# A first strip by plain products, W_out half converted in SBUF, and pieces converted in pairs

## The chip, the cores and the metric

The kernel runs on one core of one Trainium2 chip. The metric is the device time of one execution in microseconds (us); the time of a kernel is the median over several runs. A core has five instruction streams that run beside each other: TensorE (PE; its weight loads are shown as PEld), VectorE (DVE), ScalarE (ACT), GpSimd (POOL) and SyncE (SP), and 16 DMA engines that move data between HBM and the on-chip memory SBUF. Matrix products land in PSUM.

## The reference

Attention without softmax, then a two-layer network whose hidden layer is squared after a ReLU:

```python
batch, n_heads, seq, head_dim = (8, 8, 576, 64)
kv = np.einsum('bhsd,bhse->bhde', k, v)
out = np.einsum('bhsd,bhde->bhse', q, kv)
rms = np.sqrt(np.mean(out * out, axis=-1, keepdims=True) + 1e-06)
attn = out / rms * g_norm
x = attn.transpose(0, 2, 1, 3).reshape(4608, 512)     # n_tokens, d_model
h = x @ w_in                                          # d_ff = 2048
r = np.maximum(h, 0.0)
return ((r * r) @ w_out).astype(np.float32)
```

q, k, v and g_norm are float32. `w_in` (512 x 2048) and `w_out` (2048 x 512) come as float64, 8.4 MB each, so the kernel converts them to float32 by integer operations on their words before it can use them.

## The kernel before, in words

**Tokens.** The 4608 tokens are 36 tiles of 128, worked on in 9 strips of 4 tiles (512 tokens). Attention for a pair of heads of one batch is a unit (b, p), 32 in all: `transposed_query` transposes q on PE (`t_ps`, and `tr_ps` for the 64 rows of two batches that are left over), `key_value` makes k^T v (`kv_ps`) and copies it to `kvd`. Per tile, `query` multiplies (`x_ps`), squares (`sq`), takes the root mean square on ACT and DVE and writes `x_n`; `features` transposes `x_n` (`xt_ps`) into `xT`.

**Products.** Both layers are done per strip by a scheme of 7 products of half-size blocks in place of 8 (Strassen-Winograd). `up(s, g, p)` is product p (order 1, 2, 6, 5, 7, 3, 4) of group g of four; it needs sums of blocks of W_in (slots of the SBUF tile `w_in`: 11, 21, 12, 22 and the sums S1, S2, S4) and of xT (`x_t`, made by `sums_x`). `combine` copies a PSUM bank to `snap` on ACT or adds it up on DVE; the hidden blocks are `gt`. `down(s, p, i)` is half i of product p of the second layer; its operand `w_blk` is streamed in blocks of 1 MB from `w_out`, a scratch tensor in HBM that holds the 7 block sums of the converted W_out. Banks: A (two buffers), B and C.

**Weights.** They arrive in 32 pieces of 512 KB (`raw`, three buffers), 16 of W_in and 16 of W_out. `convert_piece` makes two words per piece on ACT (L154, L169) and joins them in four DVE instructions (L155, L158, L164, L170), then asks for the next piece. The sums of W_in's blocks and of W_out's blocks are made on POOL (`sums_in` L183 and L174, `sums_out` L174); `sums_out` stores one row block of all 7 sums to `w_out` (L200).

**Order.** Each engine runs its instructions in the order in which the program writes them. The loop at the end writes strip 0's attention, then 28 `up` steps of strip 0 with the conversions spread between them by `convert(n)`; all conversions are written ahead of the first `down` of strip 0, and after that three `w_blk` loads. `attend(n)` spreads the next strip's attention over a strip's steps. All loads and stores but two tiny ones are issued from SP, in order; an issue whose buffer is not free holds up what stands behind it. All of that happens once; strips 1 to 8 only repeat `up`, `down` and attention.

Of the kernel before, what the change touches and what calls it, by code (L numbers as in the profile page):

```python
# [19 lines left out]
def kernel(  # L20
# [49 lines left out]
    qkv_pool = ctx.enter_context(tc.tile_pool(name="qkv", bufs=2))  # L70
    rest_pool = ctx.enter_context(tc.tile_pool(name="rest", bufs=NP))
# [6 lines left out]
    xc_pool = ctx.enter_context(tc.tile_pool(name="xc", bufs=1))  # L78
    snap_pool = ctx.enter_context(tc.tile_pool(name="snap", bufs=1))
    dram = ctx.enter_context(tc.tile_pool(name="dram", bufs=1, space=bass.MemoryType.DRAM))  # L80
    conv = ExitStack()
    raw_pool = conv.enter_context(tc.tile_pool(name="raw", bufs=3))
    wtmp = conv.enter_context(tc.tile_pool(name="wtmp", bufs=2))
    wt_pool = conv.enter_context(tc.tile_pool(name="wt", bufs=2))
# [7 lines left out]
    def load(b, p):  # L92
        hs = slice(2 * p, 2 * p + 2)
        half = slice(REST * (b % 2), REST * (b % 2 + 1))
        for n, src in (("k", k), ("v", v), ("q", q)):
            whole = src[b, hs, 0 : C * P].rearrange("h (sp c) d -> sp h c d", c=C)
            if n == "v":
                t = qkv_pool.tile([P, 2, C, D], FP32, name=n, tag=n)
                nc.sync.dma_start(out=t, in_=whole)
            else:  # L100

                t = qkv_pool.tile([P, C, 2, D], FP32, name=n, tag=n)
                for h in range(2):
                    nc.sync.dma_start(out=t[:, :, h, :], in_=whole[:, h])
# [10 lines left out]
    def load_next():  # L115
        u = next(to_load, None)
        if u is not None:
            load(*u)

    for _ in range(2):  # L120
        load_next()
# [26 lines left out]
    def convert_piece(i, dest):  # L148
# [27 lines left out]
    def piece_in(i):  # L176
        g, kc = divmod(i, NP)
        b = kc // KH * 2
        convert_piece(i, w_in[:, b : b + 2, kc % KH, ts(g, WN // 2)])

    def sums_in(g):
        a11, a21, a12, a22, s1, s2, s4 = (w_in[:, b, :, ts(g, WN // 2)] for b in range(7))
        nc.gpsimd.tensor_tensor(out=s1, in0=a21, in1=a22, op=ALU.add)  # L183
        minus(nc.gpsimd, s2, s1, a11)
        minus(nc.gpsimd, s4, a12, s2)
        minus(nc.gpsimd, a21, a11, a21)

    def piece_out(i):
        j, b = divmod(i, 2)
        if b == 0:  # L190
            wt[j] = wt_pool.tile([P, 7, DH], FP32, name="wt", tag="wt")
        convert_piece(NG * NP + i, wt[j][:, 2 * b : 2 * b + 2, :])

    def sums_out(j):
        b11, b12, b21, b22, t1, t2, t4 = (wt[j][:, b, :] for b in range(7))
        minus(nc.gpsimd, t1, b12, b11)
        minus(nc.gpsimd, t2, b22, t1)
        minus(nc.gpsimd, b12, b22, b12)
        minus(nc.gpsimd, t4, b21, t2)
        nc.sync.dma_start(out=w_out[:, :, j, :].rearrange("b p e -> p b e"), in_=wt.pop(j))  # L200

    conversions = []
    for g in range(NG):
        conversions += [(piece_in, NP * g + kc) for kc in range(NP)] + [(sums_in, g)]
    for j in range(FQ):
        conversions += [(piece_out, 2 * j), (piece_out, 2 * j + 1), (sums_out, j)]
# [8 lines left out]
    for _ in range(3):  # L215
        load_piece()

# [12 lines left out]
    def transposed_query(b, p):  # L230
# [6 lines left out]
        if b % 2:  # L237
            t = rest.pop(("q", b // 2, p))
# [3 lines left out]
            nc.vector.tensor_copy(qT["rest", b // 2, p], ps)  # L242

    def key_value(b, p):
# [3 lines left out]
        for c in range(C):  # L248
            nc.tensor.matmul(ps, lhsT=flat(tk[:, c]), rhs=tv[:, :, c, :], start=(c == 0), stop=False)  # L249
        nc.tensor.matmul(  # L250
            ps, lhsT=flat(rest["k", b // 2, p][half]), rhs=rest["v", b // 2, p][half], start=False, stop=True
# [6 lines left out]
        nc.vector.tensor_copy(d[D:P, D:P], ps[D:P, D:P])  # L258
        kvd[b, p] = d
        load_next()  # L260

    def query(n):
# [14 lines left out]
        sq = xn_pool.tile([P, d_model], FP32, name="sq", tag="sq")  # L277
# [40 lines left out]
    for b in range(B):  # L318
# [33 lines left out]
    B_OUT = {1: 0, 2: 2, 3: 3, 4: 6, 5: 4, 6: 5, 7: 1}  # L352
# [27 lines left out]

    def up(s, g, p):
# [6 lines left out]
        for i in range(2):  # L388
            product(p, i, lambda kc: w_in[:, A_IN[p], kc, ts(2 * g + i, P)], lambda kc: rhs[:, kc, :], KH)

        if (s, 1) not in gq:
            for q in (11, 12, 21, 22, 1):
                gq[s, q] = g_pool.tile([P, FQ, TH], FP32, name="gt", tag="gt")
        dest = {q: gq[s, q][:, 2 * g : 2 * g + 2, :] for q in (11, 12, 21, 22, 1)}

        def relu_squared(q):
            def f(b, a):
# [3 lines left out]
                if q == 12:  # L401
                    nc.vector.tensor_tensor(out=dest[1], in0=dest[12], in1=dest[22], op=ALU.add)
                    minus(nc.vector, dest[12], dest[11], dest[12])
# [8 lines left out]
    to_stream = iter([(s, p) for s in range(N_STRIP) for p in ORDER])  # L412
# [7 lines left out]
    def down(s, p, i):  # L420
# [8 lines left out]
        stream()  # L429
# [19 lines left out]
    for i in range(ready[0]):  # L449
        attend(i + 1)  # L450
        convert(i // 2 - 5)
    for s in range(N_STRIP):
        attend(ready[s])
        steps = [(1, up, (s, g, p)) for g in range(NG) for p in ORDER]
# [48 lines left out]
```

## Time and profile before

| what | value |
|---|---|
| time, median of 3 runs | 1126.4 us (1126.19 to 1126.85) |
| the profiled execution | 1126.69 us |
| its span, first to last instruction | 1124.9 us |
| PE busy | 1003.8 us (89%) |
| DVE, ACT, POOL busy | 461.5, 243.9, 61.2 us |
| moved by DMA | 128.75 MB |

The span leaves 1.8 us of the profiled execution outside. Busy shares are means over a start with conversions and a long stretch of strips, which have different limits, so the rows below are taken stretch by stretch. Windows and timelines count us from the start of the span.

### The profile page before, as it was taken

The page shows a single profiled execution, that of the slowest core. Times are in us where ns is not written, and L with a number is a line of the kernel's source. Part 1 is how long each engine was busy: PE and PEld are TensorE (multiplying, and loading weights), DVE is VectorE, ACT ScalarE, POOL GpSimd, SP SyncE. Part 2 cuts the span into 40 slices and gives each one's busy share as a digit, 9 for nine tenths or more (in the row PEclk, how much of TensorE's full clock was granted, in tenths as well). Part 3 has the DMA queues.
Part 4 walks back from the last instruction along what each step waited for, and adds up shares of the span by engine and source line. Part 5 has one row for each costly group of instructions (what it writes and reads, how often), then busy time and mean ns, then how long its engine had stood idle before and what let it go on. Part 6 is the DMA issues. An engine that isn't in the chain of part 4 may idle for free.

```text
span 1124.9 us, 12527 instructions
## 1 busy us (share of the span) xinstructions
PE 1003.8 (89%) x4960; PEld 878.9 (78%) x4960; DVE 461.5 (41%) x797; ACT 243.9 (22%) x454; POOL 61.2 (5%) x118
## 2 busy tenths in 40 slices
PE   3456920699999999999999999999999999999998
PEld 3345710588888888888888888888888888888887
DVE  0677788232442245234424342542253324512430
ACT  1423433012211221122103210321132112201200
POOL 0042235000000000000000000000000000000000
PEclk9888965799999999999999999999999999999999
DMA  7443468543334323422541354126402350044032
GB/s 187 108 130 109 132 206 270 187 164 102 87 104 137 116 71 116 145 71 64 148 169 47 74 151 156 45 63 186 161 18 64 122 178 1 11 154 135 1 112 75
DMA packets 123850, 128.75 MB, mean 114 GB/s; under 512 B 85008, under 2 KB 109584, under 8 KB 115728
## 3 DMA queue, kind: packets, MB, share of 16 engines
q1 hardware_dynamic: 123632, 127.95, 36.5%
q8 instruction: 39, 0.64, 0.2%
q14 instruction: 19, 0.16, 0.0%
q10 hardware_dynamic: 160, 0.00, 0.0%
HBM read 111.15 MB, written 16.78 MB: 114 GB/s over the span
## 4 chain that ended last, share of the span: by engine, by line
PE 84%; DVE 9%; DMA 3%; SPq 1%; POOL 1%; issue 1%; ACT 1%; DVEq 0%; POOLq 0%; ACTq 0%
PE ps_A L364 43%; PE ps_B L364 21%; PE ps_C L364 11%; PE x_ps L275 2%; PE kv_ps L249 2%; PE xt_ps L302 1%; PE t_ps L234 1%; PE kv_ps L250 1%; DMA raw<-in_moe_w_out_dram 1%; DVE w_c L155 1%; DVE w_c L158 1%; DVE w_in L170 1%; DVE gt L400 1%; DVE w_in L164 1%; DVE wt L164 1%
## 5 line engine op out<-in xcount | busy, mean ns | idle before, releaser
L364 PE MATMUL ps_A<-w_blk,gt 128*128 128x256 f32 x1152 | 259.1, 381 | 58.4 <-DMA w_blk<-w_out 58.4
L364 PEld LDWEIGHTS ps_A<-w_blk,gt 128*128 128x128 f32 x1152 | 218.0, 191 | 88.1 <-issue 58.8
L364 PE MATMUL ps_A<-x_t,w_in 128*128 128x256 f32 x864 | 206.6, 382 | 6.0 <-DVE w_in L170 5.3
L364 PEld LDWEIGHTS ps_A<-x_t,w_in 128*128 128x128 f32 x864 | 161.8, 190 | 29.7 <-DVE w_in L170 6.3
L364 PE MATMUL ps_B<-w_blk,gt 128*128 128x256 f32 x576 | 128.5, 379 | 0.0
L364 PEld LDWEIGHTS ps_B<-w_blk,gt 128*128 128x128 f32 x576 | 108.4, 190 | 14.3 <-issue 0.2
L174 DVE TENSOR_TENSOR gt<-gt 128x512 f32<-128x512 f32 (+1 forms) x54 | 69.0, 1279 | 87.4 <-PE ps_A L364 57.7
L374 ACT COPY snap<-ps_A 128x512 f32<-128x512 f32 x90 | 52.7, 585 | 203.0 <-PE ps_A L364 203.0
L364 PE MATMUL ps_A<-xT,w_in 128*128 128x256 f32 x288 | 74.1, 401 | 24.6 <-DVE w_in L170 24.6
L399 DVE TENSOR_TENSOR gt<-ps_C,snap 128x512 f32<-128x512 f32 x36 | 24.9, 692 | 160.1 <-PE ps_C L364 160.1
L364 PEld LDWEIGHTS ps_A<-xT,w_in 128*128 128x128 f32 x288 | 56.7, 201 | 34.4 <-DVE w_in L170 26.3
L400 DVE SCALAR_TENSOR_TENSOR gt<-gt 128x512 f32<-128x512 f32 x108 | 76.7, 710 | 3.7
L364 PE MATMUL ps_C<-xT,w_in 128*128 128x256 f32 x288 | 69.9, 386 | 0.0
L364 PE MATMUL ps_B<-xT,w_in 128*128 128x256 f32 x288 | 68.8, 382 | 1.2 <-ACT snap L374 1.2
L364 PE MATMUL ps_B<-x_t,w_in 128*128 128x256 f32 x288 | 68.2, 380 | 0.0
L399 DVE TENSOR_TENSOR gt<-ps_A,snap 128x512 f32<-128x512 f32 x36 | 24.9, 691 | 105.2 <-PE ps_A L364 104.7
L364 PE MATMUL ps_C<-w_blk,gt 128*128 128x256 f32 x288 | 65.1, 381 | 0.0
L364 PEld LDWEIGHTS ps_C<-xT,w_in 128*128 128x128 f32 x288 | 56.0, 195 | 8.2
L364 PEld LDWEIGHTS ps_B<-xT,w_in 128*128 128x128 f32 x288 | 53.5, 190 | 9.0 <-ACT snap L374 1.6
L364 PEld LDWEIGHTS ps_C<-w_blk,gt 128*128 128x128 f32 x288 | 53.7, 190 | 7.4 <-issue 0.2
L364 PEld LDWEIGHTS ps_B<-x_t,w_in 128*128 128x128 f32 x288 | 53.6, 190 | 6.8 <-PE x_ps L270 0.2
L280 DVE TENSOR_REDUCE ms<-sq 128x8 f32<-128x512 f32 x36 | 24.6, 684 | 80.2 <-ACT sq L278 80.1
(59 smaller groups left out, 773.6 us busy)
## 6 DMA issues: line engine op xcount, KB each, us to landing
w_blk<-w_out SPq DMA_DIRECT2D x63, 1024.0 KB, 4.9
k<-in_k_dram SPq DMA_DIRECT2D x64, 128.0 KB, 2.9
v<-in_v_dram SPq DMA_DIRECT2D x32, 256.0 KB, 3.1
q<-in_q_dram SPq DMA_DIRECT2D x64, 128.0 KB, 3.0
raw<-in_moe_w_in_dram SPq DMA_DIRECT2D x16, 512.0 KB, 4.0
raw<-in_moe_w_out_dram SPq DMA_DIRECT2D x16, 512.0 KB, 4.6
out_dram<-o_sb SPq DMA_DIRECT2D x64, 128.0 KB, 4.9
w_out<-wt SPq DMA_DIRECT2D x8, 896.0 KB, 4.9
```

Source lines behind the costliest of these rows:

```text
L155: nc.vector.tensor_scalar(out=c, in0=c, scalar1=LEAST, scalar2=MOST, op0=ALU.max, op1=ALU.min)
L158: nc.vector.tensor_scalar(out=ci, in0=ci, scalar1=3, scalar2=0x3FFFFFFF, op0=ALU.logical_shift_left, op1=ALU.bitwise_and,)
L164: nc.vector.scalar_tensor_tensor(out=dest, in0=high, scalar=-(2**30), in1=ci, op0=ALU.bitwise_and, op1=ALU.bitwise_or)
L170: nc.vector.tensor_tensor(out=dest, in0=dest, in1=r, op=ALU.add)
L174: eng.tensor_tensor(out=out, in0=a, in1=b, op=ALU.subtract)
L249: nc.tensor.matmul(ps, lhsT=flat(tk[:, c]), rhs=tv[:, :, c, :], start=(c == 0), stop=False)
L275: nc.tensor.matmul(o, lhsT=qT[b, p][:, c_b, :], rhs=kvd[b, p], start=True, stop=True)
L280: nc.vector.reduce_sum(out=ms, in_=by_head(sq), axis=AX.X)
L364: nc.tensor.matmul(bank[BANK[p]][:, i, :], lhsT=lhsT(k), rhs=rhs(k), start=p in (1, 5, 2) and i == 0 and k == 0, stop=k == n - 1, skip_gro ...
L374: nc.scalar.copy(snap[p], b)
L399: nc.vector.tensor_tensor(out=o, in0=b, in1=a, op=ALU.add)
L400: nc.vector.scalar_tensor_tensor(out=o, in0=o, scalar=0.0, in1=o, op0=ALU.max, op1=ALU.mult)
```

## The change

- Strip 0's first layer is done plainly (`up_first`: 16 steps, each four 128x512 products into one bank). Its ReLU and square are on ACT, by 128x256; it needs none of the sums of W_in's blocks. The 16 sums of W_in are made on DVE during strip 0's second layer.
- W_out is loaded in two halves of columns. The left half (8 pieces) is converted into the slots of `w_in` that later hold S1 and S2, stored to `w_out` from there, and used from there as operand of strip 0's `down` products 1 and 2. The sums of the right half are made on DVE.
- Pieces are converted in pairs, instruction by instruction for both; ACT makes the words of the next pair ahead of the pair's DVE part. `raw` and its words have four buffers.
- `w_in` is laid out with the seven blocks of a group side by side.
- q of the first four units and the left-over rows of batch 0 are loaded from POOL's queue; left-over rows are loaded per batch (three DMAs) in place of per unit; q, k, v have three buffers in place of two, the left-over rows one per kind, `o_sb` two in place of three. Two copies (`qT_rest`, half of `kvd`) go from DVE to ACT.

The core of the diff:

```diff
-    def load(b, p):
+    def load(b, p, q_eng):
-        for n, src in (("k", k), ("v", v), ("q", q)):
+        for n, src, eng in (("k", k, nc.sync), ("v", v, nc.sync), ("q", q, q_eng)):
...
+    def load_rest(b, eng):
+        half = slice(REST * (b % 2), REST * (b % 2 + 1))
+        for n, src in (("k", k), ("v", v), ("q", q)):
             if b % 2 == 0:
-                rest[n, b // 2, p] = rest_pool.tile([P, 2, D], FP32, name=f"{n}_rest", tag=f"{n}_rest")
+                rest[n, b // 2] = rest_pool.tile([P, H, D], FP32, name=f"{n}_rest", tag=f"{n}_rest")
+            eng.dma_start(out=rest[n, b // 2][half], in_=src[b, :, C * P : S].rearrange("h s d -> s h d"))
...
-    w_in = wpool.tile([P, 7, KH, FH], FP32, name="w_in")
+    w_in = wpool.tile([P, KH, NG, 7, WN // 2], FP32, name="w_in")
+    w_out_11, w_out_21 = (w_in[:, :, :, b].rearrange("p k g e -> p (k g) e") for b in (4, 5))
...
+    def convert_pieces(ids, dests):
+        for i in range(acted[0], min(ids[-1] + 3, len(sources))):
+            convert_on_act(i)
+            acted[0] = i + 1
+        now = [words.pop(i) for i in ids]
+        for c, _, _ in now:
+            nc.vector.tensor_scalar(out=c, in0=c, scalar1=LEAST, scalar2=MOST, op0=ALU.max, op1=ALU.min)
...
+        for (c, r, _), dest in zip(now, dests):
+            nc.vector.tensor_tensor(out=dest.bitcast(I32), in0=c.bitcast(I32), in1=r, op=ALU.add)
+        for _ in ids:
+            load_piece()
...
+    def pieces_out(j):
+        dest = lambda j: w_in[:, j // NG, j % NG, 4:6]
+        convert_pieces((NG * NP + j, NG * NP + j + 1), [dest(j), dest(j + 1)])
+        if j + 2 == FQ:
+            nc.sync.dma_start(out=w_out[0], in_=w_out_11)
+            nc.sync.dma_start(out=w_out[1], in_=w_out_21)
...
+    conversions = [(pieces_in, i) for i in range(0, NG * NP, 2)]
+    conversions += [(pieces_out, j) for j in range(0, FQ, 2)] + [(sums_out, j) for j in range(0, FQ, 2)]
...
+    def up_first(g, fh, i):
+        tag = "ABAC"[2 * fh + i]
+        ps = fpsum.tile([P, STRIP], FP32, name=f"ps_{tag}", tag=tag, bufs=2 if tag == "A" else 1)
+        for kc in range(NP):
+            nc.tensor.matmul(
+                ps, lhsT=w_in[:, kc % KH, g, kc // KH * 2 + fh, ts(i, P)], rhs=xt[0][:, kc, :],
+                start=kc == 0, stop=kc == NP - 1,
+            )
...
+        for th in range(2):
+            o = dest[(11, 12, 21, 22)[2 * fh + th]][:, i, :]
+            nc.scalar.activation(o, ps[:, ts(th, TH)], AF.Relu)
+            nc.scalar.activation(o, o, AF.Square)
...
     for i in range(ready[0]):
+        convert(i // 4 + 1)
         attend(i + 1)
-        convert(i // 2 - 5)
...
+        if s == 0:
+            steps = [(2, up_first, (g, fh, i)) for g in range(NG) for fh in range(2) for i in range(2)]
...
-                convert((NP + 1) * (a[1] + 1) + (i % len(ORDER)) * (NP + 1) // len(ORDER) + 1)
+                convert(5 + (3 * i + 2) // 4)
...
+            if s == 0 and i == n_up + 6:
+                for g in range(NG):
+                    sums_in(g)
```

Three places show how the instructions stand. The first is the start of POOL's stream, once its constants are set: `ident` is the identity matrix that PE's transposes need, `q`, `k_rest`, `v_rest` and `q_rest` are loads. Before:

```order
masks.py:197 MEMSET ident 128x128
masks.py:199 ISA
masks.py:199 AFFINE_SELECT ident<-ident 128x128
L255 MEMSET kvd 64x64
L256 MEMSET kvd 64x64
```

After the change:

```order
L110 DMA k_rest<-in_k_dram 64x8x64
L110 DMA v_rest<-in_v_dram 64x8x64
L110 DMA q_rest<-in_q_dram 64x8x64
L102 DMA q<-in_q_dram 128x4x64 x6
masks.py:197 MEMSET ident 128x128
masks.py:199 ISA
masks.py:199 AFFINE_SELECT ident<-ident 128x128
```

Nine loads now stand ahead of the identity matrix. The second place is the end of the conversions in SP's queue: pieces of W_out (`raw`), stores of converted blocks (`w_out`), the first loads of operand blocks (`w_blk`). Before:

```order
L142 DMA raw<-in_moe_w_out_dram 128x512 x2
L200 DMA w_out<-wt 128x7x256
L142 DMA raw<-in_moe_w_out_dram 128x512
L200 DMA w_out<-wt 128x7x256 x2
L418 DMA w_blk<-w_out 128x2048 x5
```

After the change, from the store of the left half to the store of the second pair of the right half:

```order
L204 DMA w_out<-w_in 1024x1x256
L205 DMA w_out<-w_in 1024x1x256
L102 DMA k<-in_k_dram 128x4x64 x2
L97 DMA v<-in_v_dram 128x2x256
L102 DMA q<-in_q_dram 128x4x64 x2
L140 DMA raw<-in_moe_w_out_dram 128x2x256 x2
L219 DMA w_out<-wt 128x5x256 x2
L102 DMA k<-in_k_dram 128x4x64 x2
L97 DMA v<-in_v_dram 128x2x256
L102 DMA q<-in_q_dram 128x4x64 x2
L140 DMA raw<-in_moe_w_out_dram 128x2x256 x2
L219 DMA w_out<-wt 128x5x256 x2
```

The last four pieces now stand behind stores of converted blocks and behind the loads of units. The third place is PE's stream where strip 0's second layer begins (`xt_ps` and `x_ps` are tiles of strip 1). Before:

```order
L364 MATMUL ps_A<-x_t_400,w_in 128x256 x4
L364 MATMUL ps_A<-w_blk,gt 128x256 x8
L302 MATMUL xt_ps<-ident,x_n 128x128 x4
L364 MATMUL ps_A<-w_blk,gt 128x256 x8
L275 MATMUL x_ps<-kvd,qT 128x128 x4
L364 MATMUL ps_C<-w_blk,gt 128x256 x16
```

After the change:

```order
L424 MATMUL ps_C<-xT,w_in 128x512 x4
L300 MATMUL x_ps<-kvd,qT 128x128 x4
L327 MATMUL xt_ps<-ident,x_n 128x128 x4
L390 MATMUL ps_A<-w_in,gt 128x256 x8
L300 MATMUL x_ps<-kvd,qT 128x128 x4
L390 MATMUL ps_A<-w_in,gt 128x256 x8
L327 MATMUL xt_ps<-ident,x_n 128x128 x4
L300 MATMUL x_ps<-kvd,qT 128x128 x4
L390 MATMUL ps_C<-w_in,gt 128x256 x8
```

Products 1 and 2 (`ps_A`, `ps_C`) now read their operand from `w_in`, more of strip 1's attention stands between them, and the transposes of strip 1's first tile stand ahead of the first product.

## Rows read from the trace of the kernel before

**Rows 1.** The page, part 2: PE's busy tenths in 40 slices of the span.

```profile
PE   3456920699999999999999999999999999999998
```

**Rows 2.** Windows of 20 us: stretch, length, busy us by engine, PEclk, DMA share, GB/s.

```profile
20.00:40.00 20.00, 11.48 (x61) 10.22 (x62) 5.46 (x18) 5.54 (x11) 0.00 (x0) 1.00 0.65 154
140.00:160.00 20.00, 6.93 (x35) 5.56 (x33) 17.99 (x36) 7.84 (x15) 5.59 (x7) 0.79 0.54 166
160.00:180.00 20.00, 0.00 (x0) 0.00 (x0) 17.29 (x26) 6.73 (x11) 10.73 (x13) 0.50 0.93 308
180.00:200.00 20.00, 0.00 (x0) 0.00 (x0) 13.61 (x19) 4.98 (x9) 11.18 (x22) 0.50 0.71 232
```

**Rows 3.** Chain of waits, last conversion to first second-layer product: start us, us, what.

```profile
185.83 5.63 DMA raw<-in_moe_w_out_dram
...
195.37 2.08 POOL wt L174 x3
197.48 4.05 DMA w_out<-wt
...
201.65 4.77 DMA w_blk<-w_out
...
206.55 5.27 PE ps_A L364 x16
```

**Rows 4.** Timeline of PE, second layer of strip 0: start us, us, operation.

```profile
215.55 1.05 PE L275 MATMUL x_ps<-kvd,qT 128*128 128x128 f32 x8
216.44 7.07 PE L364 MATMUL ps_C<-w_blk,gt 128*128 128x256 f32 x32
223.35 0.60 PE L302 MATMUL xt_ps<-ident,x_n 128*128 128x128 f32 x4
223.78 3.62 PE L364 MATMUL ps_A<-w_blk,gt 128*128 128x256 f32 x16
...
260.98 1.89 PE L364 MATMUL ps_A<-xT,w_in 128*128 128x256 f32 x8
```

**Rows 5.** Timeline of VectorE: one piece converted, then the next instruction.

```profile
41.96 0.42 DVE L155 TENSOR_SCALAR w_c<-w_c 128x512 f32<-128x512 f32 x1
42.41 0.43 DVE L158 TENSOR_SCALAR w_c<-w_c 128x512 int32<-128x512 int32 x1
42.87 0.69 DVE L164 SCALAR_TENSOR_TENSOR w_in<-raw,w_c 128x512 int32<-128x512 int32 x1
43.71 0.69 DVE L170 CUSTOM_DVE_ANT_0 w_in<-w_in,w_r 128x1024 uint16<-128x1024 uint16 x1
44.32 0.68 DVE L280 TENSOR_REDUCE ms<-sq 128x8 f32<-128x512 f32 x1
```

**Rows 6.** Groups by line and shape, 0 to 206 us: busy us, mean ns, idle before.

```profile
L154 ACT ACTIVATE w_c<-raw 128x512 f32<-128x512 f32 x32 | 21.4, 670 | 25.0 <-DMA raw<-in_moe_w_out_dram 22.5 <-DVE w_in L164 2.2
...
L158 DVE TENSOR_SCALAR w_c<-w_c 128x512 int32<-128x512 int32 x32 | 18.7, 583 | 1.1
...
L242 DVE COPY qT_rest<-tr_ps 128x128 f32<-128x128 f32 x4 | 1.1, 284 | 3.8 <-PE tr_ps L240 3.8
```

**Rows 7.** DMA issues, 0 to 210 us: KB each, median us from issue to landing.

```profile
raw<-in_moe_w_in_dram SPq DMA_DIRECT2D x16, 512.0 KB, 4.0
raw<-in_moe_w_out_dram SPq DMA_DIRECT2D x16, 512.0 KB, 4.6
...
q<-in_q_dram SPq DMA_DIRECT2D x20, 128.0 KB, 3.0
```

**Rows 8.** The page, part 6: the stores of the result.

```profile
out_dram<-o_sb SPq DMA_DIRECT2D x64, 128.0 KB, 4.9
```

**Rows 9.** Timeline, 31 to 49 us: first query product, strip 0's last features.

```profile
31.32 2.48 PE L275 MATMUL x_ps<-kvd,qT 128*128 128x128 f32 x16
...
48.35 0.69 ACT L303 ACTIVATE xT<-xt_ps,g_col 128x512 f32<-128x512 f32 x1 [1.23 <-PE xt_ps L302]
```

**Rows 10.** Timeline of SP's queue: one DMA issued.

```profile
2.28 0.63 SPq L108 DMA_DIRECT2D k_rest<-in_k_dram  x1
```

More of the change, by code (lines that the diff above doesn't have):

```diff
@@ L173, in minus, with pieces_in @@
     def minus(eng, out, a, b):
         eng.tensor_tensor(out=out, in0=a, in1=b, op=ALU.subtract)
-    def piece_in(i):
+    def pieces_in(i):
         g, kc = divmod(i, NP)
         b = kc // KH * 2
-        convert_piece(i, w_in[:, b : b + 2, kc % KH, ts(g, WN // 2)])
+        convert_pieces((i, i + 1), [w_in[:, kh, g, b : b + 2] for kh in range(KH)])
     def sums_in(g):
[L182 to L186, printed above, removed]
@@ L202 @@
[L202 to L206, printed above, removed]
+        a11, a21, a12, a22, s1, s2, s4 = (w_in[:, :, g, b] for b in range(7))
+        nc.vector.tensor_tensor(out=s1, in0=a21, in1=a22, op=ALU.add)
+        minus(nc.vector, s2, s1, a11)
+        minus(nc.vector, s4, a12, s2)
+        minus(nc.vector, a21, a11, a21)
@@ L213, in convert @@
             converted[0] += 1
-    for _ in range(3):
+    load_rest(0, nc.gpsimd)
+    load_piece()
+    for i in range(3):
         load_piece()
+        load_next(nc.gpsimd)
     g_col = const.tile([P, 1], FP32, name="g_col")
@@ L250, in key_value @@
         nc.tensor.matmul(
-            ps, lhsT=flat(rest["k", b // 2, p][half]), rhs=rest["v", b // 2, p][half], start=False, stop=True
+            ps, lhsT=flat(rest["k", b // 2][half, 2 * p : 2 * p + 2]),
+            rhs=rest["v", b // 2][half, 2 * p : 2 * p + 2], start=False, stop=True,
         )
@@ L257, in key_value @@
         nc.scalar.copy(d[0:D, 0:D], ps[0:D, 0:D])
-        nc.vector.tensor_copy(d[D:P, D:P], ps[D:P, D:P])
+        nc.scalar.copy(d[D:P, D:P], ps[D:P, D:P])
         kvd[b, p] = d
-        load_next()
+        if b > 0:
+            load_next()
+            if p == NP - 1 and b + 1 < B:
+                load_rest(b + 1, nc.sync)
+        elif p == 0:
+            load_next(nc.gpsimd)
     def query(n):
@@ L379, in combine, with quarters, sums_g @@
             c(b, snap[other])
+    def quarters(s, g):
+        if (s, 1) not in gq:
+            for q in (11, 12, 21, 22, 1):
+                gq[s, q] = g_pool.tile([P, FQ, TH], FP32, name="gt", tag="gt")
+        return {q: gq[s, q][:, 2 * g : 2 * g + 2, :] for q in (11, 12, 21, 22, 1)}
+    def sums_g(dest):
+        nc.vector.tensor_tensor(out=dest[1], in0=dest[12], in1=dest[22], op=ALU.add)
+        minus(nc.vector, dest[12], dest[11], dest[12])
+    def up_first(g, fh, i):
+        fc = fh * FQ + 2 * g + i
+        tag = "ABAC"[2 * fh + i]
[4 more added lines that the diff above has]
+                start=kc == 0, stop=kc == NP - 1,
+            )
+        dest = quarters(0, g)
+        for th in range(2):
+            o = dest[(11, 12, 21, 22)[2 * fh + th]][:, i, :]
+            nc.scalar.activation(o, ps[:, ts(th, TH)], AF.Relu)
+            nc.scalar.activation(o, o, AF.Square)
+        if g > 0 and fh == 1 and i == 0:
+            sums_g(quarters(0, g - 1))
     def up(s, g, p):
@@ L388, in up @@
         for i in range(2):
[L389 to L394, printed above, removed]
+            product(p, i, lambda kc: w_in[:, kc, g, A_IN[p], ts(i, P)], lambda kc: rhs[:, kc, :], KH)
+        dest = quarters(s, g)
         def relu_squared(q):
@@ L401, in f @@
                 if q == 12:
-                    nc.vector.tensor_tensor(out=dest[1], in0=dest[12], in1=dest[22], op=ALU.add)
-                    minus(nc.vector, dest[12], dest[11], dest[12])
+                    sums_g(dest)
             return f
@@ L410, in up @@
         combine(p, relu_squared(11), relu_squared(12), last, relu_squared(22))
-    to_stream = iter([(s, p) for s in range(N_STRIP) for p in ORDER])
+    to_stream = iter([(s, p) for s in range(N_STRIP) for p in ORDER][2:])
+    w_blk[0, 1], w_blk[0, 2] = w_out_11, w_out_21
     def stream():
@@ L428, in down @@
         del w_blk[s, p]
-        stream()
+        if s > 0 or p not in (1, 2):
+            stream()
         if p == 1:
```

111 lines of the change are left out of this document (58 added, 53 removed).

## The prediction

> **What bounds the kernel now.** I read the page first, then windows of 20 us, then the chain of waits, then timelines of single engines. On the page, PE is at 9 tenths or more from the ninth slice on [rows 1]: after about 225 us nothing but fewer instructions on PE can help, and the change removes none there. So its worth lies in the start. The windows show that start: in 140:160 PE has 6.93 us of work, in 160:180 and 180:200 none, while DVE has 18 to 13.6 us and POOL about 11 [rows 2]. The chain names what runs there: a piece of W_out lands (5.63 us), DVE and ACT convert it, POOL sums it (2.08), the block is stored (4.05), a 1 MB operand block is read back (4.77), and only at 206.55 does PE begin the second layer of strip 0 [rows 3]. All 32 pieces, their sums, a store and a read stand ahead of that point. From the timeline I take a landmark that both kernels reach in the same state: the first product of strip 1, at 260.98 [rows 4]. From it on both have the same PE work, so the prediction is when the changed kernel gets there.
>
> **Start of strip 0's first layer.** Before, the first query product is at 31.3 and the last features are written at 49.0, 17.7 us later [rows 9]. Changed, pieces come ahead of tokens: SP's queue starts with pieces, ACT makes four pieces' words ahead of its first copy of q, and the fourth piece lies behind about 4.3 MB of loads. Small loads moved 154 GB/s at a DMA share of 0.65 [rows 2], so some 240 GB/s full; at 240 to 290 the fourth piece is there at 16 to 18 us. The tokens follow then with three pairs converted between them; I take the first query at 29 and the 17.7 us of before: 46.5, bounds 42 and 52. Four of the 16 pairs are converted by then. This stage gains next to nothing.
>
> **POOL's queue.** Nine loads stand ahead of `ident`. The trace of before has no load from POOL. Below, one costs what SP takes for one, 0.63 us [rows 10]: 6 us. Above, one holds POOL as long as q takes to land, 3.0 us [rows 7]: 27 us. I take 1.3, near SP's: 12 us, hidden behind the 16 to 18 us until ACT is free; at 27 it would delay the start by some 11. The Trainium skill ("DMA: Bandwidth & Descriptors", section "Issuing engines are not separate DMA queues") says that loads from several engines share the same 16 DMA engines and that only issue time is saved; by it the move gains SP eight issues, about 5 us of queue, and no bandwidth, and no run here shows a load from POOL yet.
>
> **Conversion, the term that decides.** One piece occupies DVE from 41.96 to 44.32, 2.36 us, of which part is waiting for the piece's own result (0.84 between the third and fourth start, where an instruction that waits for nothing follows after 0.61) [rows 5]. In pairs these gaps close: 2 x (0.35 + 0.36 + 0.61 + 0.61) = 3.9 and small gaps, 4.1 us a pair (bounds 3.9 and 4.7, two single ones). But with four buffers a pair's loads start only when the pair two back is through: 0.1 until SP issues, 0.6 for the second issue, about 4.3 to land (4.0 and more [rows 7]; two at once), ACT's two words of the first piece and the first of the second (0.67 each [rows 6]), then DVE for the rest of the pair, 3.75. That is about 10.2 us for two pairs, and ACT's ReLUs ahead of a word add 0.8: 11.0, so 5.5 us a pair, and not 4.1. Eight such pairs (rest of W_in, left half) take 44 us. The last four carry sums on DVE too: 8 of 128x256 a pair. DVE shows 0.69 for 512 columns [rows 5] and 0.28 for 128 [rows 6], so about 0.36 from start to start: 2.9 us, 7.0 a pair, and three pairs of hidden-block sums of 1.2: 31.6 us. From 44.5 (the last tile's `x_n`) that is 44.5 + 44 + 31.6 = 120.1. The last four pieces stand in SP's queue behind 2 MB of left-half stores and behind units; I add 3 us (bounds 0 and 8): 123. Before, the last piece was through on DVE when POOL took it, at 195.37 [rows 3]. Part of the difference is that POOL no longer runs beside DVE: L158 takes 0.583 us in the mean of this stage [rows 6], against the 0.43 of one with POOL idle [rows 5].
>
> **The plain product.** It is 64 products of 512 columns for 112 of 256, so 55.3 us in place of 48.4 by columns (a 7-product step's 16 records of before take half of 3.46 [rows 4]; no 512-column product is shown): 7 more on PE. PE then has 55 and some 10 of attention in the 76 us until the conversions end, so I cost it at nothing; without that cover it is 7 us. ACT has 64 operations of 128x256 (about 0.4 each, 26 us) and words for 20 pieces (2 x 0.67 each, 27 us), with copies near 60 of the 76: hidden, but not by much.
>
> **Into the second layer.** PE's stream puts the transposes of strip 1's first tile ahead of product 1, and that tile's `x_n` stands on DVE behind all conversions. So product 1 starts not with the last ReLU but after 123 + 3: 126. Products 1 and 2 take 6.91 each, with three query products of 0.89 and three transposes of 0.43 between them [rows 4]: 17.8, so product 6 starts at 143.8, in place of 223.78 [rows 4]. It needs `w_blk`: last store at about 124, and in the chain of before 8.8 us from the last store to landing of the block [rows 3]: 133, or 140 with the backlog of DMA (below). Products 1 and 2, which need no block, cover it with 4 us to spare. The five products left take 34.6: strip 1 at 178.4. In this time DVE makes `x_t` and the 16 sums of W_in, 20 x 0.61 = 12 us, begun by about 146: 20 us of cover.
>
> **What I cost at nothing.** From strip 1 on: the two copies on ACT (0.3 us or less each, ACT at 20 us of each 100 there by its 22% of the span), merged left-over loads (asked for two to three units early), third q, k, v buffers, layout of `w_in` (same element counts; cover is PE, which sets the pace). Two `o_sb` buffers: a store lands 4.9 us after issue [rows 8] and a buffer is wanted again two products, 13.8 us, later.
>
> **Sum.** 260.98 - 178.4 = 82.6 us. The profiled execution took 1126.69, so 1044.1; it stands 0.3 above the median, so **1044 us**.
>
> **Rivals.**
> Conversion at DVE's own pace: if loads land early enough, pairs take 4.1 and the last pieces do not wait: 8 x 1.4 + 3 = 14 us less, 1030. For it: SP issues less per unit. Against: in the chain of before a piece was waited for 5.63 us even with DVE half idle [rows 3].
> DMA engines bound: from 88 us, 12.9 MB remain until the last store (left stores, four pieces, right stores, four units). At 308 GB/s for a share of 0.93 [rows 2] weights move at 331 full, units at 240: 43 us full, 46.5 at 0.93, last store landed at 135, block at 140, just hidden. If the share holds at 0.71 as in 180:200 [rows 2], 61 us: block at 155, 11 late: 1055. It decides from a share of about 0.86 down.
> POOL late: nine loads of 3.0, the start 11 us later: 1055. For it speaks that DVE runs conversions beside. The Trainium skill ("SBUF — State Buffer", section "SBUF: two separate sides") warns of this: a load from POOL waits while DVE runs operations that take the shared port, 620 ns growing to about 3100; an estimate by that is nine times 3.1, 28 us. Against: DVE's first conversion cannot begin before a piece has landed, some 6 us in.
> Slower than before: the stores of the result. If a store landed only after 13.8 us instead of 4.9 [rows 8], two `o_sb` buffers would hold up DVE or ACT, and with them PE's banks, in every strip. To lose 83 us over 8 strips each must lose over 10, so two reuses of 5 us: landing beyond 19 us. Nothing in the rows speaks for it.
>
> **How the numbers follow.** Forecast 0.47 (its own range 1036 to 1051), DVE's pace 0.2, DMA bound 0.16, POOL late 0.13, slower 0.03, no change 0.01. The range runs from DVE's pace to beyond the two late ones: 1030 to 1060, which leaves out half of the first, about 0.1, some 0.06 of the late ones, and the 0.04. A measurement here tells 0.2%, about 2.3 us, from no change: faster 0.96, same 0.01, slower 0.03.
>
> **What would show it.** Right: PE's first `up_first` product near 46, conversions ending on DVE near 123, product 1 near 126 behind a transpose that waited for DVE, the wait for `w_blk` gone or under 3 us, strip 1 near 178, and from there 863.9 us to the end of the span, as before (1124.9 less 260.98). Wrong: `ident` after 20 us (POOL); PE waiting for `w_blk` by over 5 us (DMA); a distance between conversion pairs near 4.1 or above 7; or a strip of the later ones that takes longer than before.

## The result, and the profile after

| kernel | median of runs | ratio to before, 95% interval |
|---|---|---|
| before | 1126.3 us (1124.58 to 1126.85) | |
| after | 1052.3 us (1050.87 to 1052.72) | 0.9343 (0.9327 to 0.9359) |

The profiled execution took 1050.87 us, its span 1049.1. Against the 1044.1 forecast for a profiled execution that is 6.8 us more. PE's busy tenths in 40 slices, from part 2 of the page, answer to [rows 1]:

```profile
PE   3499799999999999999999999999999999999998
```

PE has 9 tenths in the third and fourth slices, falls to 7 in the fifth (105 to 131 us) and stays at 9 from the sixth on, before from the ninth. Windows of the changed kernel (columns as in [rows 2]):

```profile
0.00:20.00 20.00, 4.08 (x16) 3.29 (x17) 4.40 (x9) 4.96 (x7) 11.59 (x35) 1.00 0.94 217
40.00:60.00 20.00, 12.01 (x37) 6.81 (x36) 16.07 (x40) 10.06 (x21) 0.00 (x0) 0.70 0.40 121
60.00:80.00 20.00, 20.00 (x48) 8.93 (x47) 12.76 (x28) 14.48 (x33) 0.00 (x0) 1.00 0.96 242
80.00:100.00 20.00, 19.96 (x70) 10.49 (x69) 17.64 (x38) 17.22 (x40) 0.00 (x0) 1.00 0.94 294
100.00:120.00 20.00, 15.20 (x64) 8.41 (x64) 14.98 (x36) 9.71 (x27) 1.16 (x8) 1.00 1.06 319
120.00:140.00 20.00, 14.23 (x60) 10.30 (x61) 15.25 (x40) 9.38 (x25) 0.00 (x0) 0.83 1.03 286
```

The hole of [rows 2] from 160 to 200, in which PE had nothing, is gone. What is left of it lies between 100 and 133. PE's timeline there, at the first query and at the first and last landmark:

```profile
30.62 2.05 PE L300 MATMUL x_ps<-kvd,qT 128*128 128x128 f32 x16
...
50.52 1.09 PE L327 MATMUL xt_ps<-ident,x_n 128*128 128x128 f32 x4 [5.85 <-DVE x_n L316]
52.39 5.26 PE L424 MATMUL ps_A<-xT,w_in 128*128 128x512 f32 x8 [0.78 <-ACT xT L328]
57.49 3.60 PE L424 MATMUL ps_B<-xT,w_in 128*128 128x512 f32 x8
...
124.05 0.66 PE L295 MATMUL x_ps<-kvd,qT_rest 128*64 128x128 f32 x2 [6.64 <-ACT kvd L278]
124.64 4.98 PE L424 MATMUL ps_C<-xT,w_in 128*128 128x512 f32 x8
...
132.23 0.66 PE L327 MATMUL xt_ps<-ident,x_n 128*128 128x128 f32 x4 [1.72 <-DVE x_n L316]
132.73 3.62 PE L390 MATMUL ps_A<-w_in,gt 128*128 128x256 f32 x16
...
150.53 7.07 PE L390 MATMUL ps_A<-w_blk,gt 128*128 128x256 f32 x32
...
185.07 1.89 PE L390 MATMUL ps_A<-xT,w_in 128*128 128x256 f32 x8
```

Strip 1 begins at 185.07 instead of 260.98 [rows 4], 75.9 us earlier. From there to the end of the span it is 864.0 us, before 863.9: the strips behind are unchanged, and all of the gain lies ahead of this landmark.

The wait of 6.64 us is put down to a copy of `kvd` on ACT. ACT's own timeline shows what that copy stood behind:

```profile
109.12 0.67 ACT L152 ACTIVATE w_c<-raw 128x512 f32<-128x512 f32 x1 [4.52 <-DMA raw<-in_moe_w_out_dram]
...
119.64 0.66 ACT L152 ACTIVATE w_c<-raw 128x512 f32<-128x512 f32 x1 [5.43 <-DMA raw<-in_moe_w_out_dram]
...
123.50 0.19 ACT L277 COPY kvd<-kv_ps 64x64 f32<-64x64 f32 x1
123.70 0.21 ACT L278 COPY kvd<-kv_ps 64x64 f32<-64x64 f32 x1
```

ACT waited 5.43 us for a piece of W_out, and `kvd`, whose matrix product had long ended, stood in line behind the words of two pieces and the ReLUs of a bank. So PE waited for a load, though the row names ACT. DMA issues of the first 130 us (columns as in [rows 7]):

```profile
raw<-in_moe_w_in_dram SPq DMA_DIRECT2D x16, 512.0 KB, 5.2
raw<-in_moe_w_out_dram SPq DMA_DIRECT2D x16, 512.0 KB, 5.2
w_out<-wt SPq DMA_DIRECT2D x6, 640.0 KB, 8.2
...
w_out<-w_in SPq DMA_DIRECT2D x2, 1024.0 KB, 8.1
q<-in_q_dram SPq DMA_DIRECT2D x13, 128.0 KB, 5.1
q<-in_q_dram POOLq DMA_DIRECT2D x8, 128.0 KB, 9.4
```

A piece landed 4.0 and 4.6 us after its issue before [rows 7], now 5.2, and stores of converted blocks take over 8 (4.05 in the chain of before [rows 3]).

### The profile page after: what moved, and what is told of

Same layout as the page of the kernel before. It is cut to its first block, busy times and chain, and to the rows that moved or that the text cites. A ratio compares the mean times of both kernels' runs of the same rounds, so it can differ in the third digit from the quotient of the medians.

```text
span 1049.1 us, 12212 instructions
## 1 busy us (share of the span) xinstructions
PE 1002.4 (96%) x4864; PEld 855.6 (82%) x4864; DVE 424.3 (40%) x769; ACT 263.4 (25%) x546; POOL 18.4 (2%) x81
## 4 chain that ended last, share of the span: by engine, by line
PE 88%; DMA 5%; DVE 3%; ACT 2%; issue 1%; SPq 0%; DVEq 0%; ACTq 0%
PE ps_A L390 45%; PE ps_B L390 22%; PE ps_C L390 11%; PE x_ps L300 2%; DMA raw<-in_moe_w_in_dram 2%; PE kv_ps L268 2%; DMA w_out<-wt 2%; PE xt_ps L327 2%; PE t_ps L253 1%; DMA raw<-in_moe_w_out_dram 1%; PE kv_ps L269 1%; PE ps_A L424 1%; ACT w_c L152 1%; DVE wt L186 1%; ACT raw L155 0%
## 5 line engine op out<-in xcount | busy, mean ns | idle before, releaser
L390 PE MATMUL ps_A<-w_blk,gt 128*128 128x256 f32 x1120 | 249.9, 379 | 0.0
L390 PE MATMUL ps_A<-x_t,w_in 128*128 128x256 f32 x768 | 182.4, 380 | 0.6 <-DVE gt L450 0.6
L390 PEld LDWEIGHTS ps_A<-x_t,w_in 128*128 128x128 f32 x768 | 143.8, 190 | 20.4 <-DVE gt L450 1.0
L451 DVE SCALAR_TENSOR_TENSOR gt<-gt 128x512 f32<-128x512 f32 x96 | 66.4, 692 | 3.3
L390 PE MATMUL ps_B<-xT,w_in 128*128 128x256 f32 x256 | 61.1, 382 | 0.0
L390 PE MATMUL ps_A<-xT,w_in 128*128 128x256 f32 x256 | 60.9, 381 | 0.0
L390 PE MATMUL ps_B<-x_t,w_in 128*128 128x256 f32 x256 | 60.5, 379 | 0.0
L390 PE MATMUL ps_C<-xT,w_in 128*128 128x256 f32 x256 | 60.5, 379 | 0.0
L305 DVE TENSOR_REDUCE ms<-sq 128x8 f32<-128x512 f32 x36 | 24.6, 684 | 77.8 <-ACT sq L303 77.7
L390 PEld LDWEIGHTS ps_C<-xT,w_in 128*128 128x128 f32 x256 | 48.6, 190 | 6.6
L390 PEld LDWEIGHTS ps_A<-xT,w_in 128*128 128x128 f32 x256 | 48.2, 190 | 6.8
```

Source lines behind the costliest of these rows:

```text
L305: nc.vector.reduce_sum(out=ms, in_=by_head(sq), axis=AX.X)
L390: nc.tensor.matmul(bank[BANK[p]][:, i, :], lhsT=lhsT(k), rhs=rhs(k), start=p in (1, 5, 2) and i == 0 and k == 0, stop=k == n - 1, skip_gro ...
L451: nc.vector.scalar_tensor_tensor(out=o, in0=o, scalar=0.0, in1=o, op0=ALU.max, op1=ALU.mult)
```

## The experiments

All times are medians, beside runs of the kernel before on the same chip (1126.3 to 1126.8 us). The kernel before differs by 0.6 us between the three chips used, so smaller differences between runs are not read. "Product 1" and "strip 1" are the starts of those PE rows in each profile.

| run | us | ratio, 95% interval | product 1 | strip 1 |
|---|---|---|---|---|
| after | 1052.31 | 0.9343 (0.9327 to 0.9359) | 132.73 | 185.07 |
| e_q_sp | 1052.61 | 0.9346 (0.9332 to 0.9360) | 133.95 | 186.29 |
| e_defer_units | 1047.77 | 0.9301 (0.9285 to 0.9317) | 129.32 | 181.67 |
| e_late_store | 1044.65 | 0.9273 (0.9259 to 0.9287) | 126.34 | 178.69 |
| e_both | 1046.57 | 0.9294 (0.9280 to 0.9308) | 126.06 | 180.88 |
| e_pool_sums | 1052.32 | 0.9338 (0.9320 to 0.9357) | 135.22 | 187.56 |
| e_single | 1054.26 | 0.9350 (0.9326 to 0.9375) | 135.88 | 188.23 |
| e_stream_all | 1062.24 | 0.9424 (0.9404 to 0.9443) | 142.26 | 196.08 |
| b_plain | 1105.65 | 0.9819 (0.9792 to 0.9846) | 184.22 | 239.66 |
| e_late_single | 1052.58 | 0.9341 (0.9323 to 0.9359) | 132.27 | 186.70 |
| e_best | 1042.33 | 0.9252 (0.9238 to 0.9267) | 124.17 | 176.95 |
| e_start3 | 1051.21 | 0.9332 (0.9317 to 0.9346) | 133.01 | 185.36 |
| e_best3 | 1041.49 | 0.9256 (0.9229 to 0.9283) | 122.84 | 175.62 |

### Who issues the first loads

```diff
-    load_rest(0, nc.gpsimd)
+    load_rest(0, nc.sync)
-        load_next(nc.gpsimd)
+        load_next()
```

> The changed kernel with q of the first four units and batch 0's left-over rows asked for from SP again. Theory A, the DMA engines are the limit of the start (share 0.94 in the first 20 us), so who issues does not matter: the first up_first product stays within 1.5 us of 52.4 and the time within 2 us of 1052. Rival B, SP's issuing is the limit there: eleven more issues of 0.63 us push the pieces back by about 7 us, so the first product comes near 59 and the time near 1059. Rival C, loads from POOL are late ones (9.4 us to landing): the first product comes some 3 us earlier, 1049.

No difference (1052.61 against 1052.31). The first first-layer product stands at 53.36 instead of 52.39. Landings do move: of the loads issued in the first 20 us, q lands 5.4 us after issue (9.4 from POOL) and pieces 6.0 (8.1), and the fourth piece's words begin at 19.85 instead of 23.07. The first layer starts no earlier for it, so the move of the issues is worth nothing here. The Trainium skill ("DMA: Bandwidth & Descriptors", section "Issuing engines are not separate DMA queues") says that issuing from several engines saves only the time to issue; the two times agree with it.

### The queue at the end of the conversions

The first edit asks for three units and the left-over rows of batch 2 only behind the first block loads. The second moves the left half's two stores (1 MB each) there. The third does both.

```diff
-            nc.sync.dma_start(out=w_out[0], in_=w_out_11)
-            nc.sync.dma_start(out=w_out[1], in_=w_out_21)
...
                 for _ in range(3):
                     stream()
+                nc.sync.dma_start(out=w_out[0], in_=w_out_11)
+                nc.sync.dma_start(out=w_out[1], in_=w_out_21)
```

> The changed kernel with the loads of batch 2's first three units and its left-over rows asked for after strip 0's first operand blocks, so that no unit stands ahead of the last two pieces. Theory A, the last conversions wait for a full DMA queue: one unit less (about 3.3 us) ahead of pieces 31 and 32 and three less ahead of the last stores, strip 1's first product at 181 to 182 instead of 185.1, 1049. Rival B, DVE's pairs and sums set the pace and the transfers are hidden: strip 1 stays at 185, 1052.

> The changed kernel with the two 1 MB stores of W_out's left half asked for after strip 0's first operand blocks instead of ahead of the last four pieces. Theory A, the DMA queue: the last four pieces land up to 6.4 us earlier, until DVE's 7.0 us a pair is the limit; last sums near 124 instead of 128.2, strip 1 at 180 to 181, 1047 to 1048. Rival B, DVE sets the pace: strip 1 stays at 185, 1052. Rival C, the sums of W_in, which overwrite the stored block, now wait for the late stores and hold up strip 1: later than 185.

> The two edits above together: neither the left half's stores nor batch 2's units stand ahead of the last pieces. Theory A: DVE's own pace is then the limit, from 93.4 us four pairs of 7.0 with three hidden-block sums, last sums at 124 to 125, strip 1 near 180, 1047; the two gains do not add up in full. Rival B: 185 and 1052.

Either edit alone brings the last pieces in earlier and shortens the time, by 4.5 and 7.7 us. (At the landmark it is 3.4 and 6.4; the profiled execution of after lies 1.4 below its median.) In e_late_store DVE hardly waits for pieces in this stretch (0.82 and 0.17 us); its timeline has the first instruction of three of the last four pairs 6.43 us apart:

```profile
102.14 0.76 DVE L167 TENSOR_SCALAR w_c<-w_c 128x512 f32<-128x512 f32 x2
108.57 0.76 DVE L167 TENSOR_SCALAR w_c<-w_c 128x512 f32<-128x512 f32 x2
115.00 0.42 DVE L167 TENSOR_SCALAR w_c<-w_c 128x512 f32<-128x512 f32 x1
```

and PE waits 0.80 us for `kvd`, in place of 6.64, and 2.89 ahead of product 1, in place of 1.72:

```profile
118.03 0.40 PE L292 MATMUL x_ps<-kvd,qT_rest 128*64 128x128 f32 x2 [0.80 <-ACT kvd L275]
...
125.85 0.66 PE L324 MATMUL xt_ps<-ident,x_n 128*128 128x128 f32 x4 [2.89 <-DVE x_n L313]
126.34 3.62 PE L387 MATMUL ps_A<-w_in,gt 128*128 128x256 f32 x16
```

The same amount of data moves; only its place in the queue differs. e_both came as expected (1046.57 against 1047, strip 1 at 180.88). What was not expected is that e_late_store alone is faster: it came 2.4 us below the low end of its expectation, since a pair takes DVE 6.43 us and not 7.0. So e_both is 1.9 us slower than one of its parts, although its conversions end no later. PE's rows show where:

```profile
125.15 1.12 PE L326 MATMUL xt_ps<-ident,x_n 128*128 128x128 f32 x4 [3.47 <-DVE x_n L315]
126.06 6.09 PE L389 MATMUL ps_A<-w_in,gt 128*128 128x256 f32 x16
```

The first half of product 1 takes 6.09 us here and 3.62 above; the window 125 to 135 has a granted clock of 0.70, where e_late_store has 1.00. A wait of 3.47 us on PE was followed by 2.5 us of slow products, and that is more than the 0.7 us by which its transpose is earlier.

### The other parts of the change

e_pool_sums makes the block sums on POOL again (`nc.vector` to `nc.gpsimd` in `sums_in` and `sums_out`). e_single converts the pieces of a pair one after the other. e_stream_all lets strip 0's products 1 and 2 wait for streamed blocks:

```diff
-    to_stream = iter([(s, p) for s in range(N_STRIP) for p in ORDER][2:])
-    w_blk[0, 1], w_blk[0, 2] = w_out_11, w_out_21
+    to_stream = iter([(s, p) for s in range(N_STRIP) for p in ORDER])
```

b_plain is the kernel before with `up_first` as strip 0's first layer and `sums_in` put behind it; strip 0's `sums_x`, then unused, go, and the conversions are spread over the 16 steps. From its edit:

```diff
-        steps = [(1, up, (s, g, p)) for g in range(NG) for p in ORDER]
+        if s == 0:
+            steps = [(2, up_first, (g, fh, i)) for g in range(NG) for fh in range(2) for i in range(2)]
...
-                convert((NP + 1) * (a[1] + 1) + (i % len(ORDER)) * (NP + 1) // len(ORDER) + 1)
+                convert(6 + 2 * i)
```

> All block sums are made on POOL again, as in the kernel before; everything else as after the change (1052.3 us). Theory A (the last pairs of pieces wait for loads, not for DVE): DVE loses 2.7 us of sums a pair, but a pair still waits for its pieces, so product 1 stays at 131 to 134; POOL needs 8 x 0.86 = 6.9 us a pair, runs behind and stores the last rows some 6 us later, and the first streamed block, not waited for until now, becomes due within 1 to 3 us of its landing: 1050 to 1056. Theory B (DVE's volume sets the pace): pairs at 3.8 to 4.5 us, conversions end 8 us or more earlier, 1040 to 1045. Theory C (POOL beside DVE slows DVE, as the 0.583 against 0.43 of before): pairs of the right half take longer on DVE, L170's 0.35 spacing grows by a third or more, and the time is 1056 or more.

> Pieces are converted one after the other on DVE, four instructions each, instead of instruction by instruction for two; words are still made ahead. Theory A (loads set the pace of most pairs): the 2 x 2.36 = 4.7 us of two single pieces against the 3.75 of a pair is hidden for the pairs that wait, so at most the four last count: 1052 to 1056. Theory B (DVE sets the pace): 12 pairs x 0.97 = 11.6 us later, 1062 to 1065.

> Strip 0's products 1 and 2 of the second layer read their operand from streamed blocks as the others do, not from the slots of w_in (the left half is still converted there and stored). If the two products that need no block hide the last store and the reading back, as the prediction says: product 1 waits from 132.7 to the landing of the first block, at 143 to 148, and the time is 1062 to 1068. If the blocks were there anyway: 1052.

> The kernel before (1126.4 us) with one part of the change: strip 0's first layer by plain products with ReLU and square on ACT, the sums of W_in's blocks on POOL after product 1's and 2's place in the second layer; conversions single, W_out's sums on POOL, all else as before. Theory A (the chain piece, conversion, POOL sum, store, read back sets the start): PE's start of the second layer moves little, only by what W_in's sums cost POOL's queue, 1118 to 1126. Theory B (DVE's volume sets the start, 17 to 18 of 20 us busy there): about 23 us of DVE work of the Strassen-Winograd first layer leave it, second layer 15 to 23 us earlier, 1103 to 1112.

**Sums on POOL: no change** (1052.32). Both effects expected are in the trace. DVE loses the sums, but works slower while POOL adds (98.27 to 106.3; POOL is idle from 113.9 to 118.1), and then waits for pieces. From DVE's timeline:

```profile
102.81 1.81 DVE L170 TENSOR_SCALAR w_c<-w_c 128x512 int32<-128x512 int32 x2
104.54 2.34 DVE L176 SCALAR_TENSOR_TENSOR w_c<-raw,w_c 128x512 int32<-128x512 int32 x2
106.80 1.28 DVE L181 CUSTOM_DVE_ANT_0 wt<-raw,w_c 128x1024 uint16<-128x1024 uint16 x2
113.08 0.74 DVE L167 TENSOR_SCALAR w_c<-w_c 128x512 f32<-128x512 f32 x1 [5.00 <-ACT w_c L152]
...
115.43 0.76 DVE L170 TENSOR_SCALAR w_c<-w_c 128x512 int32<-128x512 int32 x2
```

The same two instructions of L170 take 1.81 us beside POOL and 0.76 without it. The Trainium skill ("SBUF — State Buffer", section "SBUF: two separate sides") states that DVE and GpSimd share one pair of ports that one of them holds at a time; these rows agree with it. It costs nothing here because 5.00 us of waiting for the next piece follow. (Its product 1 at 135.22 is later than the 131 to 134 expected; the profiled execution was the slowest of its four, 1053.72.)

**Single pieces: not told apart from after** (the intervals overlap), as theory A had it for loads that set the pace.

**Blocks instead of `w_in`: 9.9 us slower.** PE waits for the first block:

```profile
142.26 5.10 PE L390 MATMUL ps_A<-w_blk,gt 128*128 128x256 f32 x16 [9.82 <-DMA w_blk<-w_out]
```

This is product 1's block; in the changed kernel the first block is product 6's, and SP's queue there has

```profile
132.89 2.35 SPq L219 DMA_DIRECT2D w_out<-wt  x2
141.32 1.28 SPq L469 DMA_DIRECT2D w_blk<-w_out  x3
```

The quickest of these three loads landed 4.7 us after its issue, at about 146.0, and product 6 begins at 150.53. So the two products that need no block cover store and load with some 4.5 us to spare, close to the 4 of the prediction.

**The plain strip alone: 21 us of the 74**, the time that theory B gave (its four runs lie between 1104.77 and 1110.43). The second layer begins at 184.22 instead of 206.55 [rows 3].

> As the run with the left half's stores after the first block loads (1044.65 us), but with pieces converted one at a time on DVE. Theory A (without the late loads DVE sets the pace of the last pairs, which are 6.43 us apart there): each of the last four takes 1.0 more, product 1 at 130 to 131, 1048 to 1050. Theory B (PE's own work covers it): 1044 to 1046.

e_late_single is e_single on top of e_late_store: 7.9 us slower than that, more than the 3 to 5 expected. With loads out of the way a pair takes 7.4 us (first pieces at 105.11, 112.50 and 119.86), not 6.43. The second of the last four pairs already begins 3.0 us later (105.11 against 102.14), the first layer 1.1 of it; the rest adds another 2.9, so product 1 is 5.9 late. The other 2 are PE's again: it waits 4.42 us, and the first half of product 1 takes 5.71. So the conversion in pairs is worth little in the changed kernel and 8 us once its pieces come in time.

### A faster version

e_best is e_late_store with strip 1's first transposes behind the first half of product 1, not ahead of it. e_start3 is the changed kernel with three pairs converted ahead of strip 0's last tile, not four. e_best3 has all three edits.

```diff
-        convert(i // 4 + 1)
+        convert(min(i // 4 + 1, 3))
...
+                if i < n_up:
+                    to = min(to, next(j for j in range(ready[0], goal) if slices[j][0] is features))
```

> As the run with the left half's stores after the first block loads (1044.65 us), and the transposes of strip 1's first tile stand behind the first half of product 1 on PE, not ahead of it. Theory A (product 1 waits only because that tile's x_n stands behind all conversions on DVE): the 2.9 us that PE waited there go, product 1 at 123.0, product 6 near 141, strip 1 near 175.8: 1041 to 1042.5. Theory B (the wait comes back behind it, at the transposes or at a block): 1044 to 1045.5.

> The changed kernel (1052.3 us), with three pairs of pieces converted ahead of strip 0's last tile instead of four: the fourth pair, 3.75 us on DVE, no longer stands ahead of that tile's x_n, for which PE waits 5.85 us. First product of the first layer at 48 to 49 instead of 52.4. Theory A (the late pieces set the end of the conversions, whatever the start): product 1 stays at 131 to 133, 1050 to 1053. Theory B (PE's own work from the first product on sets it): the 3.8 us stay, 1047 to 1049.

> Three edits at once: left half's stores after the first block loads, product 1 ahead of strip 1's first transposes, three pairs ahead of the last tile. Theory A (with the loads out of the way PE's own work, 95% busy from the first product to product 1, sets the start): first product at 48 to 49, product 1 at 118.5 to 120, 1036.5 to 1039.5. Theory B (DVE's conversions, or ACT's words, set it from the first tile on): product 1 as without the third edit, near 123, 1041 to 1042.5.

e_best beats after by 10.0 us. e_start3 begins the first layer at 49.43 and still reaches product 1 only at 133.01: the late piece's words begin on ACT at 119.82, against 119.64, and PE waits for `kvd` until 124.27, against 124.05, whatever the start. In e_best3 the start is 47.77, 4.6 us ahead of e_best, but only 1.3 us are left at product 1. Its PE rows show where the rest goes:

```profile
47.77 5.36 PE L421 MATMUL ps_A<-xT,w_in 128*128 128x512 f32 x8 [0.78 <-ACT xT L325]
...
100.97 0.47 PE L256 MATMUL tr_ps<-ident,q_rest 128*128 128x128 f32 x1 [4.51 <-ACT qT L252]
101.24 5.84 PE L421 MATMUL ps_A<-xT,w_in 128*128 128x512 f32 x8
```

PE now overtakes ACT, which is 17.15 us busy from 80 to 100, waits 4.51 us for a copy and goes on with a slow product. The two versions can't be told apart (1041.75 to 1042.77 and 1040.94 to 1045.82). A fifth `raw` buffer, which would test what the loads' distance costs, was not tried.

## Why the prediction was right, and where its sizes were off

**The number.** The forecast was 1044, the time is 1052.3: 74.0 us of gain where 82.3 were forecast. That lies inside 1030 to 1060, but 1.3 us beyond the 1036 to 1051 that the prediction gave its own sum; it was the room left for the two rivals at 1055 that took it in. Neither rival came as told: `ident` was early, and the DMA rival's block was in time, though its full queue made pieces late. Of the prediction's signs, the order of events, the wait of a transpose ahead of product 1, no wait for `w_blk` and an unchanged rest came true; the times of the first layer, the end of the conversions and product 1 were each 6 to 7 us late.

**Where the gain is.** At the landmark the change brings 75.9 us. b_plain reaches it at 239.66: 21.3 us come from the plain strip. e_stream_all shows 11.0 us at the landmark (196.08 against 185.07) for operands that need no store and read-back. The remaining 43.6 us are conversions that end earlier: b_plain's last DVE instruction of a piece ends at 172.1, the changed kernel's last sum of a piece at 128.1, 44.0 earlier:

```profile
171.42 0.69 DVE L170 CUSTOM_DVE_ANT_0 wt<-wt,w_r 128x1024 uint16<-128x1024 uint16 x1
```

(The changed kernel's last sums are among DVE's rows below.) Of the 44 some 21 us are an estimate for five more pieces converted by 50 us (eight against three, at b_plain's 4.2 us a piece), and 23 for the 24 others, 77.8 us from 50.29 to 128.1 or 3.24 a piece. By DVE's rows b_plain has it busy 83.8 and idle 37.9 us from 50.4 to 172.1, the changed kernel 59.7 and 18.1 from 50.3 to 128.1: 24 us less work and 20 less waiting. Taken back one at a time, pairs and the place of the sums cost 2 us and nothing. How much the buffers, the order of the loads and the stores give was not separated, so for the largest part of the gain the place is shown and the cause is not.

**The start of the first layer**, 46.5 forecast, came at 52.39, 0.4 beyond the bound of 52. The rate held: from 2.3 us, when the transfers begin, to 23.07 the engines moved 246 GB/s. But by then 5.1 MB had moved, not the 4.3 that the forecast put ahead of the fourth piece, whose words waited for its landing until 23.07 on ACT, not 16 to 18:

```profile
18.34 0.67 ACT L152 ACTIVATE w_c<-raw 128x512 f32<-128x512 f32 x1 [7.43 <-DMA raw<-in_moe_w_in_dram]
...
23.07 0.66 ACT L152 ACTIVATE w_c<-raw 128x512 f32<-128x512 f32 x1 [3.51 <-DMA raw<-in_moe_w_in_dram]
```

This delay mostly did not reach the start: the first query stands at 30.62 (forecast 29), and e_q_sp, whose fourth piece is 3.2 us earlier, starts no earlier. The step that failed is "the 17.7 us of before" behind it. From the first query to the last features it is 21.7 us, because the fourth pair stands on DVE ahead of the last tile's `x_n` (the 5.85 us wait above). With that pair taken away, in e_start3, it is 17.3:

```profile
32.07 3.78 PE L300 MATMUL x_ps<-kvd,qT 128*128 128x128 f32 x16
...
49.43 5.38 PE L424 MATMUL ps_A<-xT,w_in 128*128 128x512 f32 x8 [0.78 <-ACT xT L328]
```

**POOL's nine loads** were issued in 0.7 to 0.8 us each, and `ident` was set at 8.13, against 12 (bounds 6 and 27); near the lower bound, and off the path (with the left-over rows SP is spared eleven issues, not eight):

```profile
1.28 0.83 POOL L110 DMA_DIRECT2D k_rest<-in_k_dram  x1 [0.82 <-POOLq L556]
...
3.46 3.73 POOL L102 DMA_DIRECT2D q<-in_q_dram  x5
...
8.13 0.22 POOL masks.py:197 MEMSET ident<- 128x128 f32 x1
```

DVE's first conversion begins only at 6.94, so these rows do not test the rule on ports that the prediction weighed.

**A pair and the eight pairs.** A pair with nothing to wait for takes 3.75 us (first instructions at 50.29 and 54.04), below the lower bound of 3.9. Eight pairs took 43.1 us, 50.29 to 93.41, against 44:

```profile
50.29 0.75 DVE L167 TENSOR_SCALAR w_c<-w_c 128x512 f32<-128x512 f32 x2
...
93.41 0.42 DVE L167 TENSOR_SCALAR w_c<-w_c 128x512 f32<-128x512 f32 x1
...
127.42 0.75 DVE L186 TENSOR_TENSOR wt<-w_in,wt 128x256 f32<-128x256 f32 x2
128.10 0.68 DVE L415 TENSOR_TENSOR gt<-gt 128x512 f32<-128x512 f32 x1
...
129.42 0.68 DVE L305 TENSOR_REDUCE ms<-sq 128x8 f32<-128x512 f32 x1
```

The size is right, the reason only in part: the gaps are ACT's words, and ACT waited not only for loads (3.70 and 1.77 us) but also for PE's bank (3.1), since its ReLUs stand ahead of the words.

**The last four pairs and what lies behind stores.** Forecast 31.6 + 3; measured 36.0 (93.41 to 129.42). With the left half's stores moved it is 29.6 (93.46 to 123.03): DVE's own part was 2.0 smaller than the term and the wait 6.4 instead of 3, within its bounds of 0 and 8. This is the DMA rival's mechanism, but not at its place: the block was in time by 4.5 us, the pieces were late. The queue was not idle either, at a DMA share of 1.03 to 1.06.

**The plain product at nothing.** (A step of the 7-product scheme has 8 records, not the 16 of the prediction [rows 4]; its 48.4 stands.) The prediction gave PE 65 us of work in 76 and called it covered. PE is busy 47.56 of 47.60 us from 52.4 to 100, so there was no free time there; the cost was paid in that stretch and hidden because the late pieces made PE wait afterwards. In the faster versions that cover shrinks; a kernel that tests its price then was not run.

**Into strip 1.** Product 1 at 132.73 stands 3.3 behind the last conversion work (forecast 3), behind a transpose that waited for DVE as described. From product 1 to product 6 it is 17.8 us and from there to strip 1 34.5, as forecast; no wait for `w_blk`; the sums of W_in on DVE cost nothing.

**The sum.** Start +5.8 (the last tile's `x_n`: 50.29, not 44.5), eight pairs -0.9, last pairs -2.0, late pieces +3.4, product 1 +0.3: 6.6 of the 6.7 us at the landmark. The rivals: DVE's pace holds only in e_late_store and its followers, for the last pairs, POOL was not late, the result's stores changed nothing (864.0 us behind the landmark).

## What to carry to other kernels

When loads, stores and prefetches share one queue, write down what each is needed for: two stores that only the next strip reads, put ahead of the last loads, cost 7.7 us here though no byte more was moved. A wait that the trace puts on an in-order engine (ACT's copy) may be a load's: look at what stands ahead of the named instruction on that engine. An edit that is worth nothing beside a late load (pairs, 2 us or less) can be worth 8 us once that load is on time, so test parts again after the bound has moved.

## What the runs showed of the hardware

After a wait of PE the products that followed were often slow, and the granted clock in such windows lay below 1.00: 5.26 us against 3.60 after 5.85 us of waiting, 4.98 against 3.70 after 6.64, 5.71 and 6.09 against 3.62 after 4.42 and 3.47. The last wait alone does not decide it: after 2.89 in e_late_store the product took 3.62, but in e_start3 one took 5.38 after waits of 1.23, 2.10 and 0.78 close together. In the slow cases the idle cost 1.3 to 2.5 us more than itself, a term that the sum did not have. The window 125:135 of e_both shows a mean of 0.70 between the two levels, 1.2 and 2.4 GHz.

Loads that POOL issued took 0.70 to 0.83 us each of its time. They landed 9.4 us after issue, against 5.4 for the q that SP issued in e_q_sp's first 20 us; but the pieces beside them also landed later, 8.1 against 6.0, so the longer landing is not shown to be POOL's own.
